# Attention, expert layer and SwiGLU on one core: stacks of k and q as one tile each, p*v in one block

## The chip, the cores and the metric

The kernel runs on one core of one Trainium2 chip. The time is device microseconds of that core, one launch. Before the change it is 815.24 us, the median of 3 runs (814.94 to 817.06).

## The reference

Three layers follow one another, all in float32. The change lies in the first.

```
# attention: q, k, v are (2, 8, 768, 64), proj is (64, 6)
q_bits = (q @ proj > 0); k_bits = (k @ proj > 0)      # 6 sign bits each
mask   = bucket(q_bits)[:, None] == bucket(k_bits)[None, :]
scores = where(mask, q @ k.T / 8, -1e9)
attn   = softmax(scores);  x = attn @ v               # per batch and head
# experts: 1536 tokens, 8 experts of capacity 192, greedy assignment by x @ w_gate
x[mask_e] = relu(x[mask_e] @ w1[e]) @ w2[e]
# SwiGLU with an RMS norm
out = (silu(xn @ w_gate) * (xn @ w_val)) @ w_out
```

## The kernel before

One core does the layers in turn. In the attention stage two heads that lie side by side form a pair of heads; there are 8 of these (`NPAIR`), p = 0 to 7. A unit u is one head's 128 queries against its 768 keys; a pair of heads takes 12 units, alternately head 0 and head 1, and the loop at L601 makes 96 of them (`NU`) in order. The engines' programs are in the order in which the code is written; each engine takes its own in that order, and what stands behind a waiting instruction on its engine waits too.

One pass of the loop issues: the exponent of unit u+1 on ScalarE (`expo`), six transposes of unit u's probabilities on TensorE (`transp`, L361) with two copies out of PSUM (ScalarE L363, VectorE L365), the four score matmuls of unit u+2 (`scores`, L336 and L339) and their minimum on VectorE (L341). Two score tiles in PSUM let scores run two units ahead. In even units `comb` (L395) joins the two heads' results of an earlier pair of units and `comb_v` scales them. The product p*v of a pair of units i (`pv`, L380) runs in two parts of 12 matmuls, one in the even unit 2i+2 and one in the odd unit 2i+3; its weights are the 64 columns of one head's v, so that the two heads' matmuls use the two halves of the array's columns. A copy on ScalarE (L385) follows the second part. After that come the fillers that the table `fill` holds for this unit.

A score matmul needs float32 accuracy from float32r operands. So q and k are split in a high and a low part, and two "stacks" of 128 rows are built for each: `s1_k` = (high, low), `s1_q` = (high, high), `s2_k` = (high, sign rows), `s2_q` = (low, sign rows). L336 multiplies the first stacks, L339 the second; the sign rows (18 of them, `NS`) carry the mask. For pairs of heads 1 to 7 the parts are made while the pair before is in its units:
- `prep_t` transposes k or q (one half at a time), ScalarE copies, GpSimd makes the high part (L285) and the low part (L286).
- `prep_d` (L302) fills the stacks: six transfers of 192 KB each for k and six for q, issued on the sync queue (SP).
- `prep_p` (L288) makes the sign rows with six matmuls and one VectorE operation (L297), `prep_s` (L315) moves them with four transfers (L320).

The table SLOTS sets in which unit of the pair of heads before these are issued, at the end of the unit: for p > 1 `prep_t` for k in units -1 and 0, `prep_d` for k in unit 0 too; `prep_t` for q in 1 and 3, `prep_d` for q in 3; `prep_p` in 5 and 6, `prep_s` in 6; `load_pair` in 7. For p = 1 the slots are 0, 0, 4, 5, 5, 6. The first scores on the new stacks are issued in unit 10.

The sync queue also issues the loads and stores of a side job (`conv_load` L242, `conv_store` L263; with the offset that stands in `CONV` they fall on units 0, 2, 4, 7, 9 and 0, 3, 5, 8, 10 of a pair of heads), weights for the next layer (`load_w`, every ninth unit from 20 on), and the stores of finished heads (L431, in unit 2). Pair 0's stacks are filled by ScalarE and VectorE (`first_t`, `first_c`, `first_l`, `first_p`).

Of the kernel before, what the change touches and what calls it, by code (L numbers as in the profile page):

```python
# [46 lines left out]
def lsh_attention__moe__swiglu_kernel(ctx, tc, q, k, v, proj, m_wg, m_w1, m_w2,  # L47
# [239 lines left out]

    def prep_p(p, half):  # L288
        sg = SG[p]
        cs = slice(half * HALF, (half + 1) * HALF)  # L290
        t = ps_m.tile([128, 512], F32, name="m")
        for n, (a, i) in enumerate(((0, 0), (0, 1), (1, 0))):
            for j, nm in enumerate("kq"):
                nc.tensor.matmul(t[:, :HALF], pjt[:, 2 * j + a], NAT[nm, p][i][:, cs],
                                 start=(n + j == 0), stop=(n + j == 3))
        n = 96 + NS
        nc.vector.tensor_scalar(sg[:n, cs], t[:n, :HALF], thr[:n], mul[:n], op0=OP.is_gt, op1=OP.mult)  # L297

    NS = 3 * NB
    SG = {}  # L300

    def prep_d(p, nm):  # L302
        nh, nl = (t.bitcast(F32) for t in NAT[nm, p])
        s1 = stk.tile([128, 2, S], F32R, name="s1_" + nm)
        s2 = stk.tile([128, 2, S], F32R, name="s2_" + nm)
        a, c = s1.bitcast(F32), s2.bitcast(F32)
        for g in range(2):
            cs = slice(g * HALF, (g + 1) * HALF)
            wh, wl = (t[64 * g:64 * g + 64].rearrange("p (h n) -> p h n", h=2) for t in (nh, nl))
            nc.sync.dma_start(a[0:64, :, cs], wh)  # L310
            nc.sync.dma_start(a[64:128, :, cs], wl if nm == "k" else wh)
            nc.sync.dma_start(c[0:64, :, cs], wh if nm == "k" else wl)
        STK[nm, p] = (s1, s2)

    def prep_s(p):  # L315
        sg = SG.pop(p).bitcast(F32)
        for j, nm in enumerate("kq"):
            c = STK[nm, p][1].bitcast(F32)
            for g in range(2):
                nc.sync.dma_start(c[64:64 + NS, :, g * HALF:(g + 1) * HALF],  # L320
                                  sg[64 * j + 32 * g:64 * j + 32 * g + NS].rearrange("p (h n) -> p h n", h=2))

    SC, PR, PTT, RS, XO = {}, {}, {}, {}, {}

    def scores(u):
        i, h = divmod(u, 2)
        p, t = divmod(i, TPB)
        k1, k2 = STK["k", p]
        q1, q2 = STK["q", p]
# [4 lines left out]
        qs = slice(place(p, t) * 128, (place(p, t) + 1) * 128)  # L334
        for n in range(2):
            nc.tensor.matmul(ps[:, n, :HALF], q1[:, h, qs], k1[:, h, n * HALF:(n + 1) * HALF],  # L336
                             start=True, stop=False)
        for n in range(2):
            nc.tensor.matmul(ps[:, n, :HALF], q2[:64 + NS, h, qs], k2[:64 + NS, h, n * HALF:(n + 1) * HALF],  # L339
                             start=False, stop=True)  # L340
        nc.vector.tensor_reduce(rs[:, h, 0:1], ps[:, :, :HALF], axis=AX.XY, op=OP.min)  # L341
        nc.vector.tensor_scalar(rs[:, h, 1:2], rs[:, h, 0:1], BIG / 2, -1.0, op0=OP.is_lt, op1=OP.mult)
        nc.vector.tensor_scalar(rs[:, h, 2:3], rs[:, h, 0:1], BIG / 2, rs[:, h, 0:1], op0=OP.is_lt, op1=OP.mult)  # L343
# [21 lines left out]
                nc.vector.tensor_copy(o[:, 0:3, :], t)  # L365
        PTT[u] = o

    def pv(i, part):
        p = i // TPB
        vt = LD["v", p]  # L370
        if part == 0:
            if i < NU // 2 - 1:
                XO[i] = ps_v.tile([128, 128], F32, name="xo")
            else:
                XO[i] = ps_s.tile([128, 2, 512], F32, name="sc")[:, 0, :128]
        xo = XO[i]
        a = (PTT[2 * i], PTT[2 * i + 1])
        for c in range(3 * part, 3 * part + 3):
            for h in range(2):
                nc.tensor.matmul(xo[64 * h:64 * h + 64], vt[:, h, chunk(p, c), :], a[h][:, c, :],  # L380
                                 start=(c == 0), stop=(c == TPB - 1))
        if part == 1:
            del PTT[2 * i], PTT[2 * i + 1]
            xt = wk.tile([128, 128], F32, name="xt", bufs=3)
            nc.scalar.activation(xt, xo, AF.Copy)  # L385
            XO[i] = xt

    XS = {}

# [63 lines left out]


    for nm in "kq":
        STK[nm, 0] = (stk.tile([128, 2, S], F32R, name="s1_" + nm), stk.tile([128, 2, S], F32R, name="s2_" + nm))

    FT = {}

# [2 lines left out]
        eng.tensor_copy(t[:, :, 1, :], t[:, :, 0, :])  # L462

    def first_t(h, nm, half):
        s1, s2 = STK[nm, 0]
        t = LD0[nm, h]
        cs = slice(half * HALF, (half + 1) * HALF)
        pt = ps_m.tile([128, 512], F32, name="m")
        for i in range(TPB // 2):
            nc.tensor.transpose(pt[:, i * 128:(i + 1) * 128],  # L470
                                t[:, half * (TPB // 2) + i].rearrange("p h d -> p (h d)"), ident)
        if nm == "k":
            nc.scalar.activation(s1[:, h, cs], pt[:, :HALF], AF.Copy)
        else:
            nc.scalar.activation(s1[:, h, cs], pt[:, :HALF], AF.Copy, scale=QS)
        FT[h, nm, half] = pt

    def first_c(h, half):
        s1, s2 = STK["k", 0]
        cs = slice(half * HALF, (half + 1) * HALF)  # L480
        nc.scalar.activation(s2[0:64, h, cs], s1[0:64, h, cs], AF.Copy)

    def first_l(h, nm, half):
        s1, s2 = STK[nm, 0]
        cs = slice(half * HALF, (half + 1) * HALF)
# [28 lines left out]
    for p in range(1, NPAIR):  # L514
        u0 = (p - 1) * TPB * 2
        slots = iter(SLOTS if p > 1 else SLOTS1)
        for nm in "kq":
            for half in range(2):
                n = u0 + next(slots)
                at(n, prep_t, p, nm, half)  # L520
            at(n, prep_d, p, nm)
        for half in range(2):
            n = u0 + next(slots)
            at(n, prep_p, p, half)
        at(n, prep_s, p)
        if p + 1 < NPAIR:
            at(n + 1, load_pair, p + 1)
# [785 lines left out]
```

## Time and profile before

| what | us |
|---|---|
| median of 3 runs | 815.24 |
| the profiled execution | 814.53 |
| its span, first to last instruction | 812.7 |
| TensorE busy (PE) | 761.3, 94% of the span |
| VectorE, ScalarE, GpSimd busy | 513.7, 398.0, 328.6 |
| share of the chain that ended last: PE, issue | 37%, 18% |

The attention stage takes the first 300 us, the routing of tokens the next 40, the expert layer goes to about 550 and the SwiGLU layer to the end. [...] An engine's busy time in a stretch is the union of its instructions; matmuls are pipelined, so their own durations overlap, and the price of a block is read from the start of one group to the start of the next. In the rows below PE is TensorE, DVE VectorE, ACT ScalarE, POOL GpSimd, and SPq the sync queue.

### The profile page before, as it was taken

The numbers are of one execution on the slowest core, as the hardware profiler recorded it, in microseconds if no ns is written. First come the engines' busy times: TensorE is split into PE (matmuls) and PEld (weight loads), VectorE is DVE, ScalarE is ACT, GpSimd is POOL, SyncE is SP. The second block draws the span as 40 slices with busy tenths as digits, with TensorE's granted clock in tenths as the row PEclk, the third lists the DMA queues.
The fourth block names the chain that finished last, engine by engine and source line by source line (L and its number), as shares of the span: only waits on it lengthen the run. The fifth ranks groups of instructions, "written<-read, shape, count | busy, mean of one in ns | idle before, by whom it ended". The sixth has DMA issues, their size and how long they took to land.

```text
span 812.7 us, 14759 instructions
## 1 busy us (share of the span) xinstructions
PE 761.3 (94%) x5317; PEld 685.2 (84%) x5317; DVE 513.7 (63%) x1342; ACT 398.0 (49%) x863; POOL 328.6 (40%) x309
## 2 busy tenths in 40 slices
PE   7999999999989983698999999999999999999997
PEld 3788777787878863498999999999999999999996
DVE  7788786889878878467787887766422332233222
ACT  3677765676766762265676776644211221121111
POOL 3278786877868720586767660000100010001001
PEclk8999999999999995699999999999999999999999
DMA  3578897989879612377777834363200110001001
GB/s 79 175 206 217 258 248 208 271 253 278 213 233 268 192 34 78 96 226 226 244 255 241 261 102 156 117 195 117 78 1 1 40 39 1 1 1 40 1 1 39
DMA packets 89770, 115.58 MB, mean 142 GB/s; under 512 B 22124, under 2 KB 68188, under 8 KB 89692
## 3 DMA queue, kind: packets, MB, share of 16 engines
q1 hardware_dynamic: 87612, 108.28, 44.8%
q0 software_dynamic: 1920, 6.29, 2.1%
q8 instruction: 44, 0.72, 0.4%
q14 instruction: 34, 0.28, 0.1%
q10 hardware_dynamic: 160, 0.00, 0.0%
HBM read 77.62 MB, written 18.87 MB: 119 GB/s over the span
## 4 chain that ended last, share of the span: by engine, by line
PE 37%; issue 18%; POOL 1%; DVE 1%; ACT 1%; POOLq 0%; ACTq 0%; DVEq 0%
PE pg L1194 6%; PE pv L1194 6%; PE py L1029 6%; PE po L1222 6%; PE ph L1005 6%; PE py L1031 3%; PE ph L1007 3%; POOL out_dram L1230 1%; PE ph L983 1%; PE py L1101 0%; DVE wl L218 0%; PE px L1061 0%; PE px L1084 0%; ACT bt L1015 0%; DVE yn L1091 0%
## 5 line engine op out<-in xcount | busy, mean ns | idle before, releaser
L1230 POOL DMA_INDIRECT out_dram<-ot,oi x12 | 11.7, 974 | 307.8 <-DVE ot L1228 306.2
L350 ACT ACTIVATE pr<-sc,rs 128x768 f32<-128x768 f32 x96 | 94.9, 989 | 50.4 <-DVE rs L343 31.6
L341 DVE TENSOR_REDUCE rs<-sc 128x1 f32<-128x768 f32 x96 | 91.5, 953 | 34.7 <-PE sc L339 34.2
L218 POOL TENSOR_TENSOR wl<-wr,wh 128x1024 fp32r<-128x1024 f32 x39 | 95.0, 2446 | 44.0 <-PE ph L983 20.9
L1203 DVE TENSOR_TENSOR a<-sg,pg 128x384 f32<-128x384 f32 x48 | 26.6, 553 | 103.1 <-ACT sg L1201 103.1
L361 PE MATMUL m<-ident,pr 128*128 128x128 f32 x576 | 83.4, 281 | 3.1 <-ACT pt L363 2.5
L380 PE MATMUL xo<-pt,ld_v 128*64 128x128 f32 x1128 | 82.9, 282 | 0.0
L1005 PE MATMUL ph<-xg,wh 128*128 128x384 f32 x256 | 75.3, 363 | 3.8 <-DVE ht L1022 3.1
L1029 PE MATMUL py<-ht,wh 128*128 128x384 f32 x256 | 76.7, 364 | 0.0
L361 PEld LDWEIGHTS m<-ident,pr 128*128 128x128 f32 x576 | 63.8, 141 | 15.1 <-issue 7.4
L380 PEld LDWEIGHTS xo<-pt,ld_v 128*64 128x64 f32 x1128 | 60.0, 137 | 18.6 <-issue 11.9
L1201 ACT ACTIVATE sg<-pg 128x384 f32<-128x384 f32 x48 | 23.5, 490 | 105.8 <-PE pg L1194 105.7
L1207 ACT ACTIVATE ah<-a 128x384 fp32r<-128x384 f32 x48 | 25.2, 525 | 99.3 <-DVE a L1204 99.3
L1194 PE MATMUL pg<-xh,gl 128*128 128x384 f32 x192 | 64.6, 336 | 0.0
L1194 PE MATMUL pg<-xl,gh 128*128 128x384 f32 x192 | 64.5, 336 | 0.0
L1194 PE MATMUL pg<-xh,gh 128*128 128x384 f32 x192 | 64.5, 336 | 0.0
L1194 PE MATMUL pv<-xh,vl 128*128 128x384 f32 x192 | 64.4, 335 | 0.0
L1194 PE MATMUL pv<-xl,vh 128*128 128x384 f32 x192 | 64.4, 335 | 0.0
L1194 PE MATMUL pv<-xh,vh 128*128 128x384 f32 x192 | 64.4, 335 | 0.0
L1031 PE MATMUL py<-ht,wl 128*128 128x192 f32 x256 | 63.7, 253 | 0.0
L215 ACT ACTIVATE wh<-wr 128x1024 fp32r<-128x1024 f32 x50 | 51.2, 1054 | 14.2 <-PE py L1029 11.4
L339 PE MATMUL sc<-s_k,s_q 82*128 82x384 f32 x192 | 49.9, 341 | 8.7 <-DMA s_q<-sg 8.7
(252 smaller groups left out, 1952.4 us busy)
## 6 DMA issues: line engine op xcount, KB each, us to landing
wr<-in_moe_w_dram SPq DMA_DIRECT2D x64, 512.0 KB, 4.7
w<-in_moe_w_gate_dram SPq DMA_DIRECT2D x12, 512.0 KB, 6.4
w<-in_moe_w_val_dram SPq DMA_DIRECT2D x12, 512.0 KB, 5.7
w<-in_moe_w_out_dram SPq DMA_DIRECT2D x12, 512.0 KB, 5.3
s_k<-nh_k SPq DMA_DIRECT2D x28, 192.0 KB, 3.4
s_q<-nh_q SPq DMA_DIRECT2D x28, 192.0 KB, 4.2
ld_v<-in_v_dram SPq DMA_DIRECT2D x8, 384.0 KB, 6.2
wg_d<-ha SPq DMA_DIRECT2D x12, 256.0 KB, 5.5
```

Of the source, the lines that this page charges most:

```text
L215: nc.scalar.activation(WH[i], WR[i], AF.Copy)
L218: (nc.gpsimd if pool else nc.vector).tensor_tensor(WL[i], WR.pop(i), WH[i], op=OP.subtract)
L339: nc.tensor.matmul(ps[:, n, :HALF], q2[:64 + NS, h, qs], k2[:64 + NS, h, n * HALF:(n + 1) * HALF], start=False, stop=True)
L341: nc.vector.tensor_reduce(rs[:, h, 0:1], ps[:, :, :HALF], axis=AX.XY, op=OP.min)
L350: nc.scalar.activation(pt, ps[:, :, :HALF], AF.Exp, scale=rs[:, h, 1:2], bias=rs[:, h, 2:3], accum_out=rs[:, h, 3:4])
L361: nc.tensor.transpose(t[:, i, :], pt[:, c * 128:(c + 1) * 128], ident)
L380: nc.tensor.matmul(xo[64 * h:64 * h + 64], vt[:, h, chunk(p, c), :], a[h][:, c, :], start=(c == 0), stop=(c == TPB - 1))
L1005: hi = lambda: nc.tensor.matmul(ph[:, :2 * CAP], wh[:, d], xg[:, d].rearrange("p a b -> p (a b)"), start=(d == 0), stop=(d == KD - 1), ski ...
L1029: hi = lambda: nc.tensor.matmul(py[d][:, :2 * CAP], wh[:, ds], ht[:, f].rearrange("p a b -> p (a b)"), start=(f == 0), stop=(f == KF - 1), ...
L1031: lo = lambda: nc.tensor.matmul(py[d][:, :CAP], wl[:, ds], ht[:, f, 0], start=False, stop=False, skip_group_check=True)
L1194: nc.tensor.matmul(t[:, :TJ], a[:, d, :], b_[:, d, :], start=(n == 0), stop=(n == 3 * KD - 1))
L1222: nc.tensor.matmul(PO[j][t], a[:, ts], b_, start=(f == 0 and n == 0), stop=(f == KG - 1 and n == 2))
```

## The change

The two stacks of k become one tile, and those of q too: `[128, 2, 2, 2, 384]` with the stack, the half of the sequence, the head and the column as axes; the high and low parts of a pair of heads become one tile as well. One transfer then fills the same rows of both stacks, and a half of both heads lies in one run of 768 floats. So `prep_d` issues four transfers instead of six, for k and for q each. `prep_d` is issued two units later: for p > 1 in unit 2 for k and 5 for q (for p = 1, in 2 and 6). The product p*v of a pair of units runs in one block of 24 matmuls, in the even unit behind `comb`, with the reciprocal of the sums (`rinv`) behind it; its copy out of PSUM becomes `pv_out`, issued in the odd unit right behind the exponent. The functions for pair 0 address the new layout and are otherwise the same.

```diff
     def prep_t(p, nm, half):
         if half == 0:
-            NAT[nm, p] = (nat.tile([128, S], F32R, name="nh_" + nm),
-                          nat.tile([128, S], F32R, name="nl_" + nm))
+            NAT[nm, p] = nat.tile([128, 2, S], F32R, name="n_" + nm)
...
+    def stack(nm):
+        return stk.tile([128, 2, 2, 2, HALF], F32R, name="s_" + nm)
+
     def prep_d(p, nm):
-        nh, nl = (t.bitcast(F32) for t in NAT[nm, p])
-        s1 = stk.tile([128, 2, S], F32R, name="s1_" + nm)
-        s2 = stk.tile([128, 2, S], F32R, name="s2_" + nm)
-        a, c = s1.bitcast(F32), s2.bitcast(F32)
+        n = NAT[nm, p].bitcast(F32)
+        STK[nm, p] = stack(nm)
+        f = STK[nm, p].bitcast(F32).rearrange("p i g h n -> p i g (h n)")
         for g in range(2):
-            cs = slice(g * HALF, (g + 1) * HALF)
-            wh, wl = (t[64 * g:64 * g + 64].rearrange("p (h n) -> p h n", h=2) for t in (nh, nl))
-            nc.sync.dma_start(a[0:64, :, cs], wh)
-            nc.sync.dma_start(a[64:128, :, cs], wl if nm == "k" else wh)
-            nc.sync.dma_start(c[0:64, :, cs], wh if nm == "k" else wl)
-        STK[nm, p] = (s1, s2)
+            r = slice(64 * g, 64 * g + 64)
+            if nm == "k":
+                nc.sync.dma_start(f[0:64, :, g], n[r, 0:1].to_broadcast([64, 2, S]))
+                nc.sync.dma_start(f[64:128, 0, g], n[r, 1])
+            else:
+                nc.sync.dma_start(f[0:64, :, g], n[r])
+                nc.sync.dma_start(f[64:128, 0, g], n[r, 0])

     def prep_s(p):
         sg = SG.pop(p).bitcast(F32)
         for j, nm in enumerate("kq"):
-            c = STK[nm, p][1].bitcast(F32)
+            c = STK[nm, p][:, 1].bitcast(F32).rearrange("p g h n -> p g (h n)")
             for g in range(2):
-                nc.sync.dma_start(c[64:64 + NS, :, g * HALF:(g + 1) * HALF],
-                                  sg[64 * j + 32 * g:64 * j + 32 * g + NS].rearrange("p (h n) -> p h n", h=2))
+                nc.sync.dma_start(c[64:64 + NS, g], sg[64 * j + 32 * g:64 * j + 32 * g + NS])
...
-    def pv(i, part):
+    def pv(i):
...
-        for c in range(3 * part, 3 * part + 3):
+        for c in range(TPB):
             for h in range(2):
                 nc.tensor.matmul(xo[64 * h:64 * h + 64], vt[:, h, chunk(p, c), :], a[h][:, c, :],
                                  start=(c == 0), stop=(c == TPB - 1))
-        if part == 1:
-            del PTT[2 * i], PTT[2 * i + 1]
-            xt = wk.tile([128, 128], F32, name="xt", bufs=3)
-            nc.scalar.activation(xt, xo, AF.Copy)
-            XO[i] = xt
+
+    def pv_out(i):
+        xt = wk.tile([128, 128], F32, name="xt", bufs=3)
+        nc.scalar.activation(xt, XO[i], AF.Copy)
+        XO[i] = xt
...
+        moves = []
         for nm in "kq":
             for half in range(2):
                 n = u0 + next(slots)
                 at(n, prep_t, p, nm, half)
-            at(n, prep_d, p, nm)
+            moves.append((n, nm))
         for half in range(2):
             n = u0 + next(slots)
             at(n, prep_p, p, half)
+        for m, nm in moves:
+            at(min(m + 2, n), prep_d, p, nm)
         at(n, prep_s, p)
...
         if u + 1 < NU:
             expo(u + 1)
+        if u % 2 == 1 and 3 <= u <= NU + 1:
+            pv_out(u // 2 - 1)
         if u < NU:
             transp(u)
         if u + 2 < NU:
             scores(u + 2)
-        if u == NU:
-            rinv(u // 2 - 1)
-            pv(u // 2 - 1, 0)
-            pv(u // 2 - 1, 1)
         if u % 2 == 0 and u >= 4:
             comb(u // 2 - 2)
             comb_v(u // 2 - 2)
-        if u % 2 == 1 and 3 <= u < NU:
+        if u % 2 == 0 and 2 <= u <= NU:
+            pv(u // 2 - 1)
             rinv(u // 2 - 1)
-        if 2 <= u < NU:
-            pv(u // 2 - 1, u % 2)
```

## Rows read from the trace of the kernel before

**Rows 1.** Busy us by engine (instructions), clock, DMA share, GB/s in three stretches.

```profile
core 0: us, PE busy (x) PEld busy (x) DVE busy (x) ACT busy (x) POOL busy (x), PEclk, DMA share, GB/s
277.50:282.37 4.87, 4.87 (x49) 4.13 (x48) 4.14 (x15) 3.58 (x8) 4.63 (x6) 1.00 0.49 135
...
97.20:102.40 5.20, 5.20 (x51) 4.47 (x50) 4.63 (x13) 4.27 (x10) 4.88 (x6) 1.00 0.94 214
...
114.90:119.77 4.87, 4.87 (x48) 4.13 (x47) 4.21 (x14) 4.03 (x9) 3.31 (x4) 1.00 0.98 313
```

**Rows 2.** Waits from 30 to 300 us, TensorE and the sync queue: total, times, longest.

```profile
PE sc L339 <- DMA s_q<-sg: 8.7, 4, 3.0
...
SPq L310 <- POOL nh_k L285: 46.8, 6, 9.3
```

**Rows 3.** TensorE's timeline from 161 to 168.4 us: start, duration, instructions merged.

```profile
162.00 0.87 PE L361 MATMUL m<-ident,pr 128*128 128x128 f32 x6
162.63 0.60 PE L336 MATMUL sc<-s_k,s_q 128*128 128x384 f32 x2
163.06 0.51 PE L339 MATMUL sc<-s_k,s_q 82*128 82x384 f32 x2
163.50 0.88 PE L380 MATMUL xo<-pt,ld_v 128*64 128x128 f32 x12
164.31 0.55 PE L278 MATMUL m<-ident,ld_k 128*128 128x128 f32 x3
164.69 0.82 PE L361 MATMUL m<-ident,pr 128*128 128x128 f32 x6
165.26 0.59 PE L336 MATMUL sc<-s_k,s_q 128*128 128x384 f32 x2
165.69 0.51 PE L339 MATMUL sc<-s_k,s_q 82*128 82x384 f32 x2
166.04 0.41 PE L395 MATMUL m<-cb,xt 128*128 128x144 f32 x2
```

**Rows 4.** Timeline at the end of the attention stage, 296 to 299 us.

```profile
296.68 0.88 PE L380 MATMUL xo<-pt,ld_v 128*64 128x128 f32 x12
296.85 0.49 ACT L363 ACTIVATE pt<-m 128x384 f32<-128x384 f32 x1 [0.70 <-PE m L361]
...
297.38 1.48 PE L380 MATMUL sc<-pt,ld_v 128*64 128x128 f32 x24
...
298.79 1.02 PE L395 MATMUL m<-cb,xt 128*128 128x144 f32 x4
```

**Rows 5.** Timeline from a unit's minimum to its exponent, 161 to 164 us.

```profile
161.05 0.96 DVE L341 TENSOR_REDUCE rs<-sc 128x1 f32<-128x768 f32 x1 [1.08 <-PE sc L339]
...
162.44 0.99 ACT L350 ACTIVATE pr<-sc,rs 128x768 f32<-128x768 f32 x1 [2.24 <-DVE lp L417]
```

**Rows 6.** Timeline around the sign rows of p=3 and p=5: VectorE, sync queue, TensorE.

```profile
111.74 0.61 SPq L312 DMA_DIRECT2D s_q<-nl_q  x1
...
112.85 0.68 DVE L297 TENSOR_SCALAR sg<-m,pm 114x384 fp32r<-114x384 f32 x1 [0.46 <-PE m L294]
...
116.22 1.71 SPq L320 DMA_DIRECT2D s_k<-sg  x2
...
123.87 0.59 PE L339 MATMUL sc<-s_k,s_q 82*128 82x384 f32 x2 [2.87 <-DMA s_q<-sg]
...
186.06 0.68 DVE L297 TENSOR_SCALAR sg<-m,pm 114x384 fp32r<-114x384 f32 x1 [0.46 <-PE m L294]
...
187.99 1.71 SPq L320 DMA_DIRECT2D s_k<-sg  x2
```

**Rows 7.** As rows 1, in stretches chosen for their transfers and their clock.

```profile
28.00:30.00 2.00, 2.00 (x22) 1.73 (x21) 1.97 (x6) 1.46 (x5) 1.10 (x2) 1.00 1.06 383
...
62.00:65.00 3.00, 3.00 (x30) 2.69 (x29) 2.40 (x10) 2.66 (x7) 2.76 (x4) 1.00 0.86 191
...
94.50:97.00 2.50, 2.50 (x26) 2.08 (x25) 2.23 (x5) 2.25 (x5) 1.61 (x3) 1.00 0.20 79
...
124.00:130.00 6.00, 6.00 (x44) 5.11 (x45) 3.33 (x10) 1.93 (x5) 1.61 (x2) 0.72 0.94 360
```

More of the change, by code (lines that the diff above doesn't have):

```diff
@@ L273, in prep_t @@
                 SG[p] = nat.tile([128, S], F32R, name="sg")
-        nh, nl = NAT[nm, p]
+        nh, nl = (NAT[nm, p][:, i] for i in range(2))
         cs = slice(half * HALF, (half + 1) * HALF)
@@ L293, in prep_p @@
             for j, nm in enumerate("kq"):
-                nc.tensor.matmul(t[:, :HALF], pjt[:, 2 * j + a], NAT[nm, p][i][:, cs],
+                nc.tensor.matmul(t[:, :HALF], pjt[:, 2 * j + a], NAT[nm, p][:, i, cs],
                                  start=(n + j == 0), stop=(n + j == 3))
@@ L327, in scores @@
         p, t = divmod(i, TPB)
-        k1, k2 = STK["k", p]
-        q1, q2 = STK["q", p]
+        k1, k2 = (STK["k", p][:, i] for i in range(2))
+        q1, q2 = (STK["q", p][:, i] for i in range(2))
+        g, qs = divmod(place(p, t), TPB // 2)
+        qs = slice(qs * 128, (qs + 1) * 128)
         if h == 0:
@@ L333, in scores @@
         ps = ps_s.tile([128, 2, 512], F32, name="sc")
-        qs = slice(place(p, t) * 128, (place(p, t) + 1) * 128)
         for n in range(2):
-            nc.tensor.matmul(ps[:, n, :HALF], q1[:, h, qs], k1[:, h, n * HALF:(n + 1) * HALF],
-                             start=True, stop=False)
+            nc.tensor.matmul(ps[:, n, :HALF], q1[:, g, h, qs], k1[:, n, h], start=True, stop=False)
         for n in range(2):
-            nc.tensor.matmul(ps[:, n, :HALF], q2[:64 + NS, h, qs], k2[:64 + NS, h, n * HALF:(n + 1) * HALF],
-                             start=False, stop=True)
+            nc.tensor.matmul(ps[:, n, :HALF], q2[:64 + NS, g, h, qs], k2[:64 + NS, n, h], start=False, stop=True)
         nc.vector.tensor_reduce(rs[:, h, 0:1], ps[:, :, :HALF], axis=AX.XY, op=OP.min)
@@ L366, in transp @@
         PTT[u] = o
-    def pv(i, part):
+    def pv(i):
         p = i // TPB
         vt = LD["v", p]
[L371 to L375, printed above, removed]
+        if i < NU // 2 - 1:
+            XO[i] = ps_v.tile([128, 128], F32, name="xo")
+        else:
+            XO[i] = ps_s.tile([128, 2, 512], F32, name="sc")[:, 0, :128]
         xo = XO[i]
-        a = (PTT[2 * i], PTT[2 * i + 1])
-        for c in range(3 * part, 3 * part + 3):
+        a = (PTT.pop(2 * i), PTT.pop(2 * i + 1))
+        for c in range(TPB):
             for h in range(2):
@@ L455, in lsh_attention__moe__swiglu_kernel @@
     for nm in "kq":
-        STK[nm, 0] = (stk.tile([128, 2, S], F32R, name="s1_" + nm), stk.tile([128, 2, S], F32R, name="s2_" + nm))
+        STK[nm, 0] = stack(nm)
     FT = {}
@@ L464, in first_t @@
     def first_t(h, nm, half):
-        s1, s2 = STK[nm, 0]
+        s1, s2 = (STK[nm, 0][:, i] for i in range(2))
         t = LD0[nm, h]
-        cs = slice(half * HALF, (half + 1) * HALF)
         pt = ps_m.tile([128, 512], F32, name="m")
@@ L472, in first_t @@
         if nm == "k":
-            nc.scalar.activation(s1[:, h, cs], pt[:, :HALF], AF.Copy)
+            nc.scalar.activation(s1[:, half, h], pt[:, :HALF], AF.Copy)
         else:
-            nc.scalar.activation(s1[:, h, cs], pt[:, :HALF], AF.Copy, scale=QS)
+            nc.scalar.activation(s1[:, half, h], pt[:, :HALF], AF.Copy, scale=QS)
         FT[h, nm, half] = pt
     def first_c(h, half):
-        s1, s2 = STK["k", 0]
-        cs = slice(half * HALF, (half + 1) * HALF)
-        nc.scalar.activation(s2[0:64, h, cs], s1[0:64, h, cs], AF.Copy)
+        s1, s2 = (STK["k", 0][:, i] for i in range(2))
+        nc.scalar.activation(s2[0:64, half, h], s1[0:64, half, h], AF.Copy)
     def first_l(h, nm, half):
-        s1, s2 = STK[nm, 0]
-        cs = slice(half * HALF, (half + 1) * HALF)
+        s1, s2 = (STK[nm, 0][:, i] for i in range(2))
         pt = FT.pop((h, nm, half))
         if nm == "k":
-            nc.vector.tensor_tensor(s1[64:128, h, cs], pt[64:128, :HALF], s1[64:128, h, cs], op=OP.subtract)
+            nc.vector.tensor_tensor(s1[64:128, half, h], pt[64:128, :HALF], s1[64:128, half, h], op=OP.subtract)
         else:
-            nc.vector.scalar_tensor_tensor(s2[0:64, h, cs], pt[0:64, :HALF], QS, s1[0:64, h, cs],
+            nc.vector.scalar_tensor_tensor(s2[0:64, half, h], pt[0:64, :HALF], QS, s1[0:64, half, h],
                                            op0=OP.mult, op1=OP.subtract)
     def first_p(h, nm, half):
-        s1, s2 = STK[nm, 0]
+        s1, s2 = (STK[nm, 0][:, i] for i in range(2))
         r = slice(64, 64 + NS)
-        cs = slice(half * HALF, (half + 1) * HALF)
         pt = ps_m.tile([128, 512], F32, name="m")
```

12 lines of the change are left out of this document (6 added, 6 removed).

## Prediction

> **What bounds the kernel now.** I read the page's shares and slices first, then the busy time of single stretches, then the waits of TensorE and of the sync queue, and last TensorE's timeline inside the attention loop, which gives the price of each block. "Unit u" below is one pass of that loop (96 in all); a pair of heads takes 12 units, and p names the pair of heads whose stacks are being prepared.
>
> The change touches only the attention stage, which ends near 300 us. TensorE is the bound there. Two units of the last pair of heads, with no preparation in them, take 4.87 us with TensorE busy throughout, VectorE 4.14 and ScalarE 3.58 [rows 1]: the reader is to see a full TensorE and a VectorE at 85%. So a TensorE saving counts at first in full, and VectorE stands next. The one wait of size that shows is of 8.7 us in four places, from 30 to 300 us, for the last transfer into the q stack (s_q<-sg) [rows 2].
>
> **Part 1: p*v in one block a pair of units.** No matmul is added or removed; what goes is switches. Block times are differences of starts in TensorE's timeline [rows 3]:
> - A block of 12 p*v matmuls (64 columns of weights each) takes 163.50 to 164.31 = 0.81 us. At the end of the stage 12 and then 24 run without a break, in 296.68 to 298.79 = 2.11 us [rows 4]; three separate blocks would take 3 x 0.81 = 2.43. Two seams gone save 0.32, so a seam is worth 0.16.
> - Entry: the second half of a unit's score matmuls (L339) takes 163.06 to 163.50 = 0.44 ahead of p*v, and 165.69 to 166.04 = 0.35 ahead of a full-width matmul: 0.09.
> - Exit: six transposes right behind p*v take 162.00 to 162.63 = 0.63, behind other transposes 164.69 to 165.26 = 0.57: 0.06.
>
> One block fewer saves 0.16 + 0.09 + 0.06 = 0.31 us. There are 48 pairs of units; the last already runs as one block. Of the other 47, the one at the end gains nothing: its second block, 296.68 to 297.38 = 0.70, now fills the time until the last probabilities are copied (ScalarE, 296.85 + 0.49 = 297.34 [rows 4]); afterwards TensorE waits there, and the 0.70 lies in the unit before. So 46 x 0.31 - 0.70 = 13.6 us less TensorE time.
>
> What it costs: the units become uneven. An odd unit is then transposes 0.63 and scores 0.78 (165.26 to 166.04), 1.41 us; two units take 4.87 - 0.31 = 4.56, so the even one 3.15. A unit's probabilities must be ready two units after its scores. The last score matmul ends 1.57 us into the unit (163.06 + 0.51, from 162.00 [rows 3]); the minimum, two small operations and the exponent take 161.05 to 162.44 to 163.43, 2.4 us [rows 5]. That leaves 4.56 - 1.57 - 2.4 = 0.6 us where there were 0.9, if VectorE and ScalarE are free. They are not always: in the stretch 97.2 to 102.4, two units with a conversion, VectorE has 4.63 of 5.20, and in 114.9 to 119.8 it has 4.21 of 4.87 and ScalarE 4.03 [rows 1]; with 0.31 off, VectorE is at 95% and 92%, and one late operation shows on TensorE. VectorE stays below TensorE in each of these, so the least lost is nothing; the most is the whole 0.31 in three of the six two-unit stretches of a pair of heads, 21 x 0.31 = 6.5 us. I take 4, nearer the upper end, since VectorE's work is bunched as well: the reciprocal's three operations move into the heavier unit.
>
> The copy of p*v (pv_out) moves behind the next exponent on ScalarE (0.99 us [rows 5]); comb reads it only after an odd unit and the next unit's transposes and scores, 1.41 + 1.35 = 2.8 us. TensorE's own work covers it; without that cover, each copy would cost what it lies over 2.8.
>
> **Part 2: the stacks.** Per pair of heads the fills fall from 12 transfers to 8. An issue takes 0.61 us [rows 6], so the sync queue is freed of 2.4 us; that matters only through what stands behind. Bytes are the same, runs twice as long (768 floats instead of 384). Does length count? In 28 to 30 us the loads of q and v, with runs of 384 floats out of HBM, go at 383 GB/s at full share, while in 62 to 65 us the stack fills, of the same run length, reach 191 at a share of 0.86 [rows 7]. Length is not what limits them, so I take no gain. The ends: nothing, or the loads' rate, with which the 2.36 MB of a pair of heads (twelve times 192 KB) would take 6.2 instead of 12.4 us.
>
> [...]
>
> **Part 3: two units later in the queue.** Now the sync queue stands still for GpSimd's split, 46.8 us ahead of k's fills alone [rows 2]. Queued behind are the conversions' loads and stores; k's move now passes unit 0's store and load and the stores of finished heads (L431), q's passes unit 3's store and unit 4's load. TensorE's list of waits has no wait for these, so no direct gain. The gain is what no longer stands between the sign rows and their issue: at p=3 the signs are ready at 112.85 + 0.68 = 113.53, but the queue still has a store, a load, a store and a weight load, and issues sg at 116.22, 2.7 us late; at p=5 it is 186.74 and 187.99, 1.25 late [rows 6]. Afterwards the transfers of units 3 and 4 are out when GpSimd frees q, and only q's four issues and one store (at p=3 the weight load too) remain. I take 2.0 us earlier, the mean of the two; the ends are 0 and 2.7.
>
> Against it: in unit 6 the whole p*v block now stands ahead of the sign matmuls (0.65 later), and units 7 to 10 are shorter by about 0.5; the deadline comes 1.1 us nearer. Net 0.9 us a pair of heads. Four waits that make 8.7 lose 0.9 each: 3.6 us gained. Ends: all 8.7 gone, or 6 x 1.1 = 6.6 added (at p=1, with other slots, no wait shows).
>
> At p=3 the stall of 2.87 us is followed by a granted clock of 0.72 in 124 to 130 us [rows 6, 7], which a shorter stall may spare: (1 - 0.72) x 6 = 1.7 us at most, left in the range.
>
> Costed at nothing: the first pair's functions have the same instructions at other addresses, behind the same loads; score matmuls read the same 384 columns as before. If a matmul had to wait for a whole stack, since it is one tile now, it would be stopped 0.43 us sooner (163.06 - 162.63: L336 instead of L339 [rows 3]) in four places: 1.7 us.
>
> **Sum.** -13.6 + 4 - 3.6 = -13.2 us on the profiled 814.53 (span 812.7 and 1.8 around it): 801.3. The median of the runs is 815.24, 0.7 higher: 802.
>
> **The rivals.**
> - VectorE and ScalarE take the saving back (0.15): the 6.5 us are lost, and the sign wait stays as it is. For it: 95% and 92% above; against: the last pair of heads has more slack, 4.14 of 4.87. -13.6 + 6.5 = -7.1: 808.
> - The signs land no sooner (0.10): what is in the rings decides, not the issue, and the nearer deadline adds 6.6. -13.6 + 4 + 6.6 = -3.0: 812. For it: at p=3 the wait ends 7.6 us after sg's first issue (116.22 to 123.87 [rows 6]); against: a share of 0.20 in 94.5 to 97 us, idle time that the unblocked queue can now use [rows 7].
> - Slower (0.05): q's fills now stand directly ahead of the signs in the rings, not 3.9 us ahead (112.35 to 116.22), and push their landing back. Place: the first L339 of each pair of heads from the second on. The gain of 9.6 us (13.6 - 4) is gone at 1.6 a place over six places; 1.1 come from the deadline, so a landing 0.5 us later than today's decides. At 1 us later, 6 x 2.1 = 12.6 and three drops of the clock at 1.7: +8.1, 823. Against: GpSimd, not the slot, sets when q starts, so q moves little.
> - The longer runs pay (0.10): fills at the rate of the HBM loads, no sign wait left, 3 lost instead of 4, the clock's drop spared: -13.6 + 3 - 8.7 - 1.7 = -21: 795. For it: only that the fills are far below the loads' rate.
>
> The forecast has 0.60, with a range of its own of 798 to 807. The range of 8 in 10, 796 to 811, leaves out half of the last rival, most of the second and the third. About 0.3% (2.4 us) can be told from no change: faster by more 0.60 + 0.14 + 0.04 + 0.10 = 0.88; within it 0.01 + 0.05 = 0.06; slower 0.01 + 0.05 = 0.06.
>
> **What would show it.** Two units of the last pair of heads at 4.56 to 4.7 us instead of 4.87; blocks of 24 p*v matmuls at 1.4 to 1.5 us; L361's waits for ScalarE among the largest of TensorE, some 4 to 7 us; L339's wait for sg near 5 us in total; the sync queue's waits for GpSimd's L285 gone; the fills' rate still near 200 GB/s; past 300 us everything only shifted. The forecast is wrong if the two units stay at 4.87 (the switch then isn't paid per block) or if sg's wait passes 12 us.

## The result and the profile after

The kernel after takes 823.56 us (median of 5 runs, 821.66 to 826.96) beside 817.06 for the kernel before on the same chip (814.94 to 818.15): a ratio of 1.0116 over the runs, 95% interval 1.0083 to 1.0149; the two medians alone give 1.008. It is slower; the forecast was 802, and the time lies outside the range of 796 to 811. The profiled execution took 826.94 us, its span is 825.2: it is 3.4 us over the median, and the sizes below are those of this one execution. One run of e9 below, of 1044.77 us at a granted clock of 0.648, is left out of its row.

The waits of TensorE and the sync queue from 30 to 300 us, in total, times and longest, for the kernel after (L341 is what L339 was, L362 what L361 was):

```profile
PE sc L341 <- DMA s_q<-sg: 20.0, 6, 5.0
PE m L362 <- ACT pr L351: 3.3, 9, 0.4
PE m L362 <- DVE pt L366: 1.5, 6, 0.3
...
SPq L431 <- DVE ri L405: 64.9, 6, 14.2
...
SPq L315 <- POOL n_q L285: 11.2, 6, 6.8
```

The wait for the sign rows is 20.0 us in six places, where it was 8.7 in four [rows 2]. The sync queue's 46.8 us in front of k's fills are gone, but it now stands 64.9 us at the stores of finished heads, ahead of k's fills.

Busy time by stretch of the kernel after (columns as in [rows 1]):

```profile
290.59:295.17 4.58, 4.58 (x49) 4.23 (x47) 4.18 (x14) 3.06 (x8) 3.96 (x6) 1.00 0.52 143
...
30.00:308.00 278.00, 252.62 (x2293) 225.19 (x2293) 216.44 (x644) 182.13 (x408) 195.09 (x202) 0.96 0.77 219
...
104.00:107.00 3.00, 3.00 (x36) 2.83 (x37) 2.07 (x9) 3.00 (x9) 2.84 (x3) 1.00 0.99 236
...
120.00:124.00 4.00, 0.00 (x0) 0.00 (x0) 1.00 (x3) 1.10 (x3) 3.48 (x4) 1.00 1.03 211
124.00:130.00 6.00, 5.79 (x44) 5.33 (x45) 2.65 (x9) 1.88 (x5) 0.81 (x1) 0.72 1.05 402
161.00:166.00 5.00, 4.62 (x35) 4.04 (x36) 2.23 (x10) 1.36 (x3) 2.75 (x3) 0.66 1.00 331
199.00:204.00 5.00, 5.00 (x40) 4.49 (x39) 2.89 (x12) 1.85 (x4) 1.96 (x2) 0.66 1.02 343
237.00:244.00 7.00, 6.45 (x38) 5.87 (x39) 2.29 (x8) 1.85 (x4) 1.17 (x1) 0.51 1.04 393
277.00:282.00 5.00, 4.91 (x37) 4.46 (x38) 2.23 (x8) 1.52 (x4) 1.45 (x2) 0.66 1.02 329
```

and the whole loop of the kernel before:

```profile
30.00:295.00 265.00, 252.99 (x2271) 213.77 (x2267) 216.34 (x643) 184.18 (x407) 195.45 (x202) 0.99 0.80 229
```

Two units of the last pair of heads take 4.58 us instead of 4.87 [rows 1]: the switch saving is there. But in 120 to 124 us TensorE does nothing at all while the DMA engines are full (a share of 1.03), and the granted clock falls from 1.00 to 0.50 of full speed for 3.4 or 6.8 us at the end of this stall and of four more, or just behind. Not every stall is followed by a fall: none comes behind the 1.26 us at p=2, nor in the kernel before behind the 3.0 us at p=6. The five stretches lose (1 - 0.72) x 6 + 3 x (1 - 0.66) x 5 + (1 - 0.51) x 7 = 10.2 us; before there was one, of 1.7 [rows 7].

Where the attention stage's 13.1 us come from (start of unit 95, the last: 295.87 before, 308.97 after; differences of the starts of units, in the same two traces):

| part | before | after | difference |
|---|---|---|---|
| start of unit 0 | 22.11 | 22.63 | +0.5 |
| units 0 to 9 of pairs of heads 0 to 6 | 198.42 | 193.47 | -4.9 |
| units 10 and 11 of these | 49.15 | 66.25 | +17.1 |
| first ten units of the last pair of heads | 24.34 | 23.90 | -0.4 |
| its 11th unit | 1.85 | 2.72 | +0.9 |

The 17.1 are 11.3 more of sign wait and 8.5 more at half clock, less 7 x 0.31 of the switches: 17.6, near the 17.1. Past 309 us things are only shifted (516.2 us to the end, 516.9 before).

What stretches the wait stands in the timelines of the kernel after around p=3, the sync queue's and GpSimd's and then TensorE's (start, duration):

```profile
99.87 0.96 SPq L431 DMA_DIRECT2D x_d<-xs  x2
100.94 0.67 SPq L312 DMA_DIRECT2D s_k<-n_k  x1
...
107.95 1.00 POOL L285 TENSOR_TENSOR n_q<-nr_q,n_q 128x384 fp32r<-128x384 f32 x1
...
108.99 0.61 SPq L315 DMA_DIRECT2D s_q<-n_q  x1
109.65 0.61 SPq L316 DMA_DIRECT2D s_q<-n_q  x1
110.31 2.19 SPq L315 DMA_DIRECT2D s_q<-n_q  x1
112.54 0.60 SPq L316 DMA_DIRECT2D s_q<-n_q  x1
113.19 1.48 SPq L263 DMA_DIRECT2D wg_d<-ha  x1
114.71 1.13 SPq L202 DMA_DIRECT2D wr<-in_moe_w_dram  x1
115.93 1.59 SPq L323 DMA_DIRECT2D s_k<-sg  x2
117.57 1.44 SPq L323 DMA_DIRECT2D s_q<-sg  x2
119.06 0.47 SPq L98 DMA_DIRECT2D ld_k<-in_k_dram  x1
...
118.66 0.60 PE L339 MATMUL sc<-s_k,s_q 128*128 128x384 f32 x2
...
124.21 0.85 PE L341 MATMUL sc<-s_k,s_q 82*128 82x384 f32 x2 [4.96 <-DMA s_q<-sg]
...
293.70 1.53 PE L380 MATMUL xo<-pt,ld_v 128*64 128x128 f32 x24
295.17 0.88 PE L362 MATMUL m<-ident,pr 128*128 128x128 f32 x6
```

q's first fill is issued at 108.99, 0.04 us after GpSimd's low part ends (108.95). The store and the load that were to be out of the way are one fewer each, but one fill's issue takes 2.19 us, and sg is issued at 115.93, hardly before the 116.22 of [rows 6].

Behind sg the queue issues the loads of the next pair of heads (L98). In 120 to 124 us they share the engines with the sign rows:

```profile
DMA packets 565, 0.84 MB, mean 211 GB/s; under 512 B 52, under 2 KB 520, under 8 KB 565
```

Fills and sign rows come in packets of 768 floats (3072 bytes) in this kernel, and only 45 of the 565 are over 2 KB. So these 4 us carry mostly the loads. How much sooner the signs would land if the loads were issued later was not tried.

### The profile page after: what moved, and what is told of

Same layout as the page of the kernel before. It is cut to its first block, busy times and chain, and to the rows that moved or that the text cites. A ratio compares the mean times of both kernels' runs of the same rounds, so it can differ in the third digit from the quotient of the medians.

```text
span 825.2 us, 14652 instructions
## 1 busy us (share of the span) xinstructions
PE 761.1 (92%) x5317; PEld 696.5 (84%) x5317; DVE 513.3 (62%) x1342; ACT 395.3 (48%) x863; POOL 328.4 (40%) x309
## 4 chain that ended last, share of the span: by engine, by line
PE 37%; issue 18%; POOL 1%; DVE 1%; ACT 1%; POOLq 0%; ACTq 0%; DVEq 0%
PE pg L1190 6%; PE pv L1190 6%; PE py L1025 6%; PE po L1218 6%; PE ph L1001 6%; PE py L1027 3%; PE ph L1003 3%; POOL out_dram L1226 1%; PE ph L979 1%; PE py L1097 0%; DVE wl L218 0%; PE px L1057 0%; PE px L1080 0%; ACT bt L1011 0%; DVE yn L1087 0%
## 5 line engine op out<-in xcount | busy, mean ns | idle before, releaser
L342 DVE TENSOR_REDUCE rs<-sc 128x1 f32<-128x768 f32 x96 | 91.6, 954 | 42.3 <-PE sc L341 41.6
L362 PE MATMUL m<-ident,pr 128*128 128x128 f32 x576 | 86.0, 282 | 5.3 <-ACT pr L351 3.6
L362 PEld LDWEIGHTS m<-ident,pr 128*128 128x128 f32 x576 | 65.2, 143 | 19.9 <-ACT pr L351 7.3
L380 PE MATMUL xo<-pt,ld_v 128*64 128x128 f32 x1128 | 78.0, 292 | 0.0
L380 PEld LDWEIGHTS xo<-pt,ld_v 128*64 128x64 f32 x1128 | 66.1, 146 | 7.3 <-issue 1.1
L341 PE MATMUL sc<-s_k,s_q 82*128 82x384 f32 x192 | 51.0, 347 | 20.0 <-DMA s_q<-sg 20.0
L364 ACT ACTIVATE pt<-m 128x384 f32<-128x384 f32 x120 | 56.1, 490 | 7.4 <-PE m L362 7.3
```

What stands on the lines that cost most here:

```text
L341: nc.tensor.matmul(ps[:, n, :HALF], q2[:64 + NS, g, h, qs], k2[:64 + NS, n, h], start=False, stop=True)
L362: nc.tensor.transpose(t[:, i, :], pt[:, c * 128:(c + 1) * 128], ident)
L364: nc.scalar.activation(o[:, 3 * half:3 * half + 3, :], t, AF.Copy)
```

## The experiments

The expectations name theories by letters. A: the later slots do the harm. B: the joined transfers of the stacks do it; D, the form of B that was left at the end: q's joined transfer holds both parts and so waits for the later one. C, and sharper H: nothing lands later in itself, TensorE only comes to its deadline earlier.

| kernel | median us | ratio to before (95%) | sign wait, us |
|---|---|---|---|
| e1 only p*v | 818.77 | 1.0050 (1.0026 to 1.0073) | 16.0 |
| e2 only stacks | 827.61 | 1.0149 (1.0113 to 1.0185) | 15.8 |
| e3 only slots | 817.00 | 1.0030 (1.0005 to 1.0055) | 9.4 |
| e4 all but slots | 832.51 | 1.0219 (1.0190 to 1.0249) | 23.4 |
| e5 after, signs by ScalarE | 840.30 | 1.0287 (1.0248 to 1.0325) | 0 |
| e6 e2, q in parts | 814.92 | 0.9987 (0.9954 to 1.0020) | 7.0 |
| e7 after, TensorE kept busy | 820.78 | 1.0059 (1.0033 to 1.0085) | 3.2 |
| e8 e1, signs by ScalarE | 842.05 | 1.0315 (1.0279 to 1.0352) | 0 |
| e9 after, q in parts | 819.44 | 1.0072 (1.0036 to 1.0109) | 15.2 |
| e10 e1, signs first | 818.85 | 1.0050 (1.0020 to 1.0080) | 12.1 |
| e11 e10, stacks, q in parts | 817.56 | 1.0035 (1.0010 to 1.0061) | 11.8 |
| e12 e11, q two units later | 806.72 | 0.9915 (0.9887 to 0.9943) | 4.2 |

The sign wait is TensorE's in each profile from 30 us to the loop's end; in e1 it includes 4.5 us that the list puts down to the load of q, in e9 3.2 put down to issue. e1 to e4 shared their runs of the kernel before, and so did e5 to e8 and e9 to e12 (medians 814.19, 815.99, 814.72); across these groups ratios are compared.

**One part each: e1, e2, e3, and e4 for the rest.** e1 is the kernel before with:

```diff
-        for c in range(3 * part, 3 * part + 3):
+        for c in range(TPB):
...
-        if 2 <= u < NU:
-            pv(u // 2 - 1, u % 2)
+        if u % 2 == 0 and 2 <= u <= NU:
+            pv(u // 2 - 1)
```

> The kernel before with p*v in one block of 24 and the copy and reciprocal moved, stacks and slots as before. Theory A (the later slots do the harm: the fills then stand behind the stores of finished heads, and the rings still hold them when the signs are issued): 6 to 10 us faster than before, two units of the last pair of heads at 4.6 to 4.85 us, the wait of the second scores for the signs between 9 and 17 us. Theory B (the longer transfers do the harm): the same as under A. Theory C (TensorE simply comes to the signs too early, whatever the transfers do): 3 us faster at most, or slower, with a sign wait of 20 us or more.

e2 is the kernel before with the new tiles and transfers, in the old slots:

```diff
-            nc.sync.dma_start(a[0:64, :, cs], wh)
-            nc.sync.dma_start(a[64:128, :, cs], wl if nm == "k" else wh)
-            nc.sync.dma_start(c[0:64, :, cs], wh if nm == "k" else wl)
...
+            else:
+                nc.sync.dma_start(f[0:64, :, g], n[r])
+                nc.sync.dma_start(f[64:128, 0, g], n[r, 0])
```

> The changed stacks (one tile, 8 transfers of 384 KB and 192 KB, runs of 768 floats) with the slots and the split p*v of before. Theory A: within 2 us of before, sign wait 6 to 10 us. Theory B: 6 to 15 us slower, sign wait over 18 us, since a 384 KB transfer stretches the issue and holds the rings. Theory C: the same as before. The rate in a stretch with fills alone: 190 to 215 GB/s if bytes decide, over 300 if the run length does.

e3 is the kernel before with the later slots (shown), e4 the kernel after without them:

```diff
-            at(n, prep_d, p, nm)
+            moves.append((n, nm))
...
+        for m, nm in moves:
+            at(min(m + 2, n), prep_d, p, nm)
```

> The kernel before with nothing changed but the slot of the fills, two units later (12 transfers, split p*v). Theory A: 8 to 18 us slower, sign wait 20 us or more, and the sync queue waiting over 40 us for the stores of finished heads. Theories B and C: within 3 us of before, sign wait 9 us or less, since the signs are no longer behind the side job's transfers.

> The changed kernel with the fills in their old slots (k in unit 0, q in unit 3). Theory A: 6 to 10 us faster than before, like p*v alone, sign wait 8 to 16 us. Theory B: slower than before by 3 us or more. Theory C: 3 us faster at most, sign wait 20 us or more.

Each part alone is slower, the stacks most (1.5%), the slots least (their interval starts at 1.0005). Theory A falls: the slots cost 0.3% alone, and with the other two parts they gain (1.0219 without them, 1.0116 with). In e3 the sync queue waits 45.3 us for VectorE at L431, and k's fills stand behind. e1 is the surprise: units 0 to 9 take 193.84 us instead of 198.42, and units 10 and 11 take 59.21 instead of 49.15. TensorE gains 4.6 us and waits them away, with more: the 10.1 longer are about 7.3 more of sign wait and 5.1 more at half clock (two stretches of 6.83 us where before had one of 3.41), less 2.2 of the switches. Where the rest of the 0.31 a pair of units went shows in e1's timeline, at the third unit of a pair of heads:

```profile
246.46 1.09 PE L361 MATMUL m<-ident,pr 128*128 128x128 f32 x6 [0.43 <-ACT pr L350]
```

The transposes wait for the exponent, as Part 1 warned.

**Is it the length of the runs, or what the transfer waits for? e6.** e2 again, with the transfer that carries both parts of q cut in two, the high part in front; the runs are still 768 floats:

```diff
-                nc.sync.dma_start(f[0:64, :, g], n[r])
+                nc.sync.dma_start(f[0:64, 0, g], n[r, 0])
                 nc.sync.dma_start(f[64:128, 0, g], n[r, 0])
+                nc.sync.dma_start(f[0:64, 1, g], n[r, 1])
```

> The stacks alone (old slots, split p*v) as in the run with the stacks alone, but q's fill again in three transfers a half, the two of the high part first, so that only the third waits for the low part; runs stay at 768 floats. Theory D (the joined q transfer must wait for GpSimd's low part too, so q's fill starts 1.6 us later and the signs behind it land later): q's first issue 1.5 us sooner against the signs than with the stacks alone, the signs land 0.8 to 1.5 us sooner, sign wait 8 to 11 us, within 0.5% of before. Theory B (long runs hold the rings): the sign wait stays at 14 us or more and the time at 1% or more over before.

Timelines at p=3, of e2 and then of e6:

```profile
113.45 1.02 POOL L285 TENSOR_TENSOR n_q<-nr_q,n_q 128x384 fp32r<-128x384 f32 x1
...
114.49 0.61 SPq L315 DMA_DIRECT2D s_q<-n_q  x1
...
130.27 0.98 PE L341 MATMUL sc<-s_k,s_q 82*128 82x384 f32 x2 [4.06 <-DMA s_q<-sg]
```

```profile
107.05 0.47 SPq L315 DMA_DIRECT2D s_q<-n_q  x1
107.10 1.02 POOL L285 TENSOR_TENSOR n_q<-nr_q,n_q 128x384 fp32r<-128x384 f32 x1
...
122.07 0.62 PE L342 MATMUL sc<-s_k,s_q 82*128 82x384 f32 x2 [2.21 <-DMA s_q<-sg]
```

In e2 the first issue comes 0.02 us after GpSimd's low part, in e6 1.07 before its end. Cutting the transfer in two is worth 1.6% (1.0149 to 0.9987); it changes its size too, but the first issue moves by 1.1 us, about the low part's own 1.02. The run length is worth nothing: the packets of 3072 bytes take 222 ns (the median of the kernel after, 30 to 300 us), those of 1536 bytes 107 before the change, nearly the same per byte; at the same share of the engines, 0.98, fills go at 218 GB/s in the kernel after (216 to 219 us) and at 215 in the kernel before (209 to 211 us). The transfers were of 192 KB before the change, and joining two of q's cost, since the joined transfer takes on the later of two waits.

**What the clock adds: e7.** The kernel after, with 14 matmuls of bf16 that nothing reads, ahead of the first L341 of each pair of heads from the third on (p = 2 to 7), so that TensorE works while it would wait:

```diff
+        if u % 12 == 0 and u > 12:
+            bt = ps_m.tile([128, 512], F32, name="m")
+            for _ in range(14):
+                nc.tensor.matmul(bt, ones_w, ones_w.unsqueeze(1).to_broadcast([128, 4, 128]), start=True, stop=True)
```

> The changed kernel with 14 extra bf16 matmuls of 512 columns (about 3 us, results unused) ahead of the first L341 of each pair of heads from the third on, where TensorE waits for the signs. Theory E (the stall costs again what the clock loses behind it): no half-clock stretch behind these places, 3 to 9 us faster than the changed kernel although TensorE has 18 us more work there. Rival (the clock's fall is hidden by other waits): as the changed kernel or up to 4 us slower.

e7's windows, over the loop, and its timeline at p=3:

```profile
30.00:303.00 273.00, 262.94 (x2379) 226.43 (x2379) 216.51 (x645) 181.58 (x408) 195.07 (x202) 0.99 0.77 223
```

```profile
120.62 3.19 PE L343 MATMUL m<-ones_w 128*128 128x512 bf16 x14
...
125.50 0.59 PE L345 MATMUL sc<-s_k,s_q 82*128 82x384 f32 x2 [1.69 <-DMA s_q<-sg]
```

With 6 x 3.0 us of work added the kernel is 0.57% faster than the kernel after (1.0116 to 1.0059), some 4.6 us; the granted clock of the loop is 0.99 instead of 0.96. The intervals of the two ratios just overlap (1.0083 to 1.0149 and 1.0033 to 1.0085). In the profiles one stretch at half clock is left of five, and it loses 1.7 us where they lost 10.2. So the stalls cost once as idle time and again in the clock behind them. The signs land no sooner (14.27 us behind the low part of q, in the kernel after 13.88).

**Is it the sync queue? e5 and e8.** The four transfers of the sign rows issued by ScalarE, in the kernel after and in e1:

```diff
-                nc.sync.dma_start(c[64:64 + NS, g], sg[64 * j + 32 * g:64 * j + 32 * g + NS])
+                nc.scalar.dma_start(c[64:64 + NS, g], sg[64 * j + 32 * g:64 * j + 32 * g + NS])
```

> The changed kernel with the sign rows' four transfers issued by ScalarE's queue instead of the sync queue. Theory F (the signs wait for the sync queue's issue and for what lies ahead of them in its rings): sign wait 0 to 6 us, 803 to 811 us. Rival G (the 16 engines are full and shared, so another queue changes little): sign wait 15 us or more, 818 us or more. If ScalarE's 2.4 us of issue hurts, its exponents start later behind unit 6 and the units 6 and 7 get longer by 1 us or more.

> p*v in one block with the stacks and slots of before, and the sign rows on ScalarE's queue. Theory F: the sign wait under 4 us, no half-clock stretch between 30 and 295 us, 803 to 809 us: what the block of p*v is worth without the sign wait (0.8 us a pair of heads against before, measured, is 6 to 7 us in all, and the 9.7 us of waits). Rival G: 815 us or more.

ScalarE's timeline in e8, and under it a line of its list of waits:

```profile
86.65 1.67 ACTq L320 DMA_DIRECT2D s_k<-sg  x2
88.36 1.64 ACTq L320 DMA_DIRECT2D s_q<-sg  x2
90.10 0.99 ACT L350 ACTIVATE pr<-sc,rs 128x768 f32<-128x768 f32 x1 [6.67 <-DMA s_k<-sg]
```

```profile
PE m L361 <- ACT pr L350: 31.6, 14, 4.6
```

The sign wait is gone in both, as theory F said, and both are slower still, by far more than its 803 to 811 us: the exponent stands behind ScalarE's wait for the sign rows and its issues (3.3 of the 6.67 us), and TensorE waits 31.6 us for exponents in e8, 30.7 in e5. Here ScalarE has other work that cannot wait. The 6.67 us show what the change of issuer cost the new one.

**Does the cure of q help the kernel after? e9.** The edit of e6 in the kernel after.

> The changed kernel with one edit: q's fill again in three transfers a half, the two of the high part first. Theory D (the joined q transfer, which waits for the low part as well, is what makes the changed kernel slower than before): 5 to 10 us faster than the changed kernel, 813 to 818 us, sign wait 12 to 16 us instead of 21. Rival (in the later slot the low part is ready anyway, so the joined transfer costs nothing there; the block of p*v is the cause): within 2 us of the changed kernel.

It gains 0.4% (1.0116 to 1.0072, with intervals that overlap) but stays slower than before. That is less than the 5 to 10 us of theory D: with the later slot the joined transfer is a part of the loss and not all of it. q's first issue comes 0.8 us before the low part's end again, yet its last issue ends later (4.2 us behind that end, before 3.2) and sg is issued no sooner (6.5, before 6.2). Why its issues stretch there was not tried.

**Is it only the deadline? e10.** e1 with the sign matmuls ahead of the p*v block in their units:

```diff
         if u % 2 == 0 and 2 <= u <= NU:
+            for f, a in [x for x in fill.get(u, []) if x[0] is prep_p]:
+                f(*a)
+            fill[u] = [x for x in fill.get(u, []) if x[0] is not prep_p]
             pv(u // 2 - 1)
```

> p*v in one block, stacks and slots as before, and the six sign matmuls of units 5 and 6 ahead of the p*v block instead of behind it. Theory H (p*v in one block is no gain because the deadline of the signs comes 1.2 us nearer): L336 of the first unit then follows the signs by 6.9 to 7.3 us as in the kernel before, sign wait 6 to 11 us, at most two half-clock stretches, 807 to 812 us, faster than before by 0.4 to 1%. Rival (the rings decide, the landing follows whatever is issued later): sign wait 14 us or more, no faster than before.

The deadline is back (at most pairs of heads the first scores come 7.15 us after the signs, before 6.87, in e1 5.7). The sign wait falls from 16.0 to 12.1 us, but the time does not: 1.0050 as in e1. Theory H, by which the deadline is all, falls. The chain of the next section says why: the signs were ready sooner (3.1 us behind the low part of q, in e1 4.1) and were used at the same time as ever. TensorE now spends the difference elsewhere: units 0 to 9 take 196.47 us, in e1 193.84, and the half clock costs 8.5 us, in e1 6.8.

**What would gain: e11 and e12.** e11 is e10 with the new stacks, q in parts, old slots. e12 moves only q's fill two units later, k's stays:

```diff
-            at(n, prep_d, p, nm)
+            if nm == "k":
+                at(n, prep_d, p, nm)
+        m = n
...
+        at(min(m + 2, n), prep_d, p, "q")
```

> As the run before, with the stacks as one tile each and q filled in three transfers a half (old slots). Theories D and H: 805 to 811 us, sign wait 4 to 10 us. Rival as there: no faster than before.

> As the run before, with q's fill two units later and k's in its old slot. If the later slot of q helps (the side job's transfers of units 3 and 4 are out before it, and the signs follow it directly): the signs' issue starts 0.3 to 1 us sooner behind the signs, sign wait under 6 us, 803 to 809 us. If q's transfers then lie directly ahead of the signs in the rings: the wait is 2 to 6 us longer than in the run before and the time 2 to 6 us.

The sync queue behind q's last fill at p=3, and the first L342, in e11 and then in e12:

```profile
112.28 0.93 SPq L263 DMA_DIRECT2D wg_d<-ha  x1
113.31 1.10 SPq L242 DMA_DIRECT2D w<-in_moe_w_val_dram  x1
114.46 0.64 SPq L263 DMA_DIRECT2D wg_d<-ha  x1
115.14 0.43 SPq L202 DMA_DIRECT2D wr<-in_moe_w_dram  x1
115.67 1.59 SPq L324 DMA_DIRECT2D s_k<-sg  x2
...
124.12 0.62 PE L342 MATMUL sc<-s_k,s_q 82*128 82x384 f32 x2 [4.05 <-DMA s_q<-sg]
```

```profile
112.06 0.63 SPq L263 DMA_DIRECT2D wg_d<-ha  x1
112.73 0.83 SPq L202 DMA_DIRECT2D wr<-in_moe_w_dram  x1
113.66 1.59 SPq L324 DMA_DIRECT2D s_k<-sg  x2
...
120.74 0.61 PE L342 MATMUL sc<-s_k,s_q 82*128 82x384 f32 x2 [1.22 <-DMA s_q<-sg]
```

e11 misses its forecast: 817.56 us and a sign wait of 11.8, so q in parts and the earlier signs are not enough together. In e12 two transfers fewer stand between q and the signs, and the signs are used 1.5 us sooner (13.09 and 11.61 us behind the low part, as in the table below). e12 takes 806.72 us, 0.85% less than the kernel before (0.57 to 1.13%), and beats both kernels. Its loop keeps the full clock:

```profile
30.00:288.00 258.00, 245.15 (x2303) 216.96 (x2302) 217.34 (x647) 182.15 (x408) 194.84 (x202) 1.00 0.82 236
```

The edit between e11 and e12 is what Part 3 forecast, for q alone, with q in parts and k where it was. Whether it needs all of that, and which of e12's differences from e9 carries more, k's slot or the order of the signs, was not tried apart.

## Why the prediction was wrong

The failed step is Part 3's "I take 2.0 us earlier ... Net 0.9 us a pair of heads ... 3.6 us gained". Counted from the moment the signs are ready, sg is first issued 1.9 us later in both kernels (means over p = 2 to 7: 1.90 and 1.93): 0.0 earlier instead of 2.0. The first L341 starts 9.8 us after the signs instead of 8.9, against a deadline that is 1.2 nearer (6.87 to 5.66 at p=3; forecast 1.1). Instead of 3.6 gained, the wait is 11.3 longer. These 14.9 us, 8.5 more at half clock and 1.9 more lost in Part 1 make 25.3 of the 25.6 us between the forecast (-13.2) and the profiled executions (+12.4).

What paces a pair of heads is a chain beside TensorE. Means over p = 2 to 7, in us from the end of GpSimd's low part of q's second half (in the first column: that end, from the start of unit 0):

| kernel | low part ends | q's first issue | q's last issue ends | sg's first issue | signs used (L339) | unit 0 to L339 |
|---|---|---|---|---|---|---|
| before | 17.62 | -1.07 | 3.24 | 6.20 | 13.24 | 30.87 |
| e1 | 18.32 | -1.06 | 3.34 | 6.13 | 13.13 | 31.45 |
| e2 | 17.62 | +0.03 | 3.82 | 7.25 | 14.44 | 32.06 |
| e6 | 17.62 | -1.07 | 2.98 | 5.93 | 12.92 | 30.54 |
| after | 18.27 | +0.13 | 3.89 | 5.99 | 13.88 | 32.15 |
| e10 | 18.26 | -1.06 | 3.28 | 6.21 | 12.94 | 31.20 |
| e12 | 18.30 | -1.06 | 3.53 | 5.44 | 11.61 | 29.91 |

The signs are used 13 us after that low part in before, e1 and e10, and unit 0 to L339 stays near 31 us, though TensorE's work in between differs. These are means: single pairs of heads go from 11.3 to 15.6 us in e1. Time saved on TensorE in between is waited away. What shortens the chain pays (e12 against e11, e6 against e2), and what lengthens it costs (e2, after).

What sets the low part is GpSimd. At p=3 of the kernel before, ScalarE has copied q's second half at 103.09 us (102.60 + 0.49), but GpSimd takes it up at 107.66, behind a conversion of the side job (L255 to L258, from 103.28 on):

```profile
106.44 1.28 POOL L258 TENSOR_TENSOR ha<-ha,sg 128x512 int32<-128x512 int32 x1
107.66 0.50 POOL L285 CAST nh_q<-nr_q 128x384 fp32r<-128x384 f32 x1
108.24 1.02 POOL L286 TENSOR_TENSOR nl_q<-nr_q,nh_q 128x384 fp32r<-128x384 f32 x1
```

Another conversion stands ahead of q's first half. Moving one of them behind the split would take 4.4 us of GpSimd's work out of the chain; it was not tried.

- **Part 1, the switches.** The mechanism was right: 1.47 us for a block of 24 (293.70 to 295.17), 4.58 for two units, the last 0.7 lost as forecast (0.9). The term "I take 4" for the lost slack was mis-sized: 35 pairs of units at 0.31 are 10.9 us in units 0 to 9, and 4.9 came: 5.9 lost, near the end of 6.5. The list of waits shows 3.3 + 1.5 of it, for the exponent and for VectorE's copy. What was overlooked is what stands behind the saving: e1 shows that, with the chain as it is, it is worth nothing. The block also makes the low part 0.70 us later (17.62 to 18.32). In unit 0 the transposes for k's second half are issued behind all 24 matmuls (at p=3 ScalarE's copy of it starts 3.73 us into the unit instead of 3.09), and GpSimd has no pause from there to the low part of q.
- **Part 2, the stacks.** "Length is not what limits them, so I take no gain" was right on length and bounded on one side only. A joined transfer has the waits of all its parts: q's first issue moves from 1.07 us before the low part's end to 0.03 behind it in e2, and L339 from 13.24 to 14.44. The prediction has no term for it. It costs 1.5% in e2, and 1.7% between e1 and e4; in the kernel after, with the later slots, taking it out gives 0.4% back (e9). "GpSimd, not the slot, sets when q starts" held; what the prediction left out is which of GpSimd's two operations.
- **Part 3, the slots.** The queue was not freed. k's fills went behind L431, which waits for VectorE (64.9 us), and q's four issues take 3.8 us from first to last (0.13 to 3.89) where six took 4.3 (-1.07 to 3.24), since one of the four stretches, at p=3 to 2.19. e12 shows that the idea can hold for q alone.
- **The clock.** "Left in the range" at 1.7 us; five drops took 10.2, 8.5 more than before. That a longer stall can cost twice should have been priced in each rival that lengthens a stall; only the slower one has it.
- **The rivals.** The slower one named the place, the price and the time (landing 1 us later: 823). The landing is 0.9 later and the time 823.56. That the number came out is in part luck: it had 12.6 us for the waits, 5.1 for the clock and 4 for the slack, where 11.3, 8.5 and 5.9 came. Its cause was given as the fills' place in the rings; the joined wait is what e6 shows for the old slots, and the fills' place was not tried apart. Its chance of 0.05 rested on "q moves little", which the joined transfer made false. The first two rivals have true parts (5.9 lost; the signs no sooner) but priced no later landing. The last rival's sum gives 794, not 795.

Of what the prediction said would show it, the bound "if sg's wait passes 12 us" was crossed at 20.0, and the fills went at 236 GB/s (104 to 107 us, where they are alone), near the 200 that it named.

## What to carry to other kernels

When transfers are joined, ask of each what it waited for: the joined one waits for the last (q's first issue came 1.1 us later in e2 than in e6). Before counting a saving on the busiest engine, follow the longest chain beside it (here split, fill, signs, landing) through one period and check that it ends sooner too. And price a stall of a few us on TensorE together with the clock that may fall behind it (10.2 us at five stalls in the kernel after).

## What the runs showed of the hardware

In the kernel after, an issue of q's joined fill on the sync queue (L315) takes 0.61 us in the median of 14, but 2.19 us at 110.31, and what stands behind it starts later by the difference (the next issue at 112.54). The engines' share is 1.07 in this stretch, but it is 0.95 in the 1.3 us before, and the next issue (112.54) takes 0.60 again with the share still over 1; so the share alone does not tell why, and the reason stays open. The fills ran at 215 to 239 GB/s with the engines' share at 0.98 to 0.99 (209 to 211 us before, 143 to 146 us after), where loads out of HBM reached 383 with the share at 1.06 [rows 7]. And 18 us of added matmuls (e7) made the kernel some 4.6 us faster, while the granted clock of the loop rose from 0.96 to 0.99.
